# Spare TensorE matmuls in the waits of a decode attention block

## The chip, the cores and the metric

One core of a Trainium2 chip. The metric is device time in microseconds (us) of one execution. Each timed execution also has a *span*, from its first to its last recorded instruction, which lies 1.3 to 2.8 us below the time for most kernels here.

## The reference, cut to what matters

One token goes through a layer norm, attention over a cache of 65536 positions, and a gated feed-forward layer.

```
x: 1 x 512.  32 query heads, 8 heads of K and V, 65536 positions of 128 each, bf16
q = layernorm(x) @ wq
p = softmax(q @ K^T / sqrt(128));  o = p @ V       # 4 query heads share one head of K and V
h = x + o @ wo
out = h + (sigmoid(n @ w_gate) * (n @ w_up)) @ w_down,  n = layernorm(h)
```

K and V are 16.8 MB per head and cache, 268 MB in all. With the weights the kernel reads 282.33 MB once.

## The kernel before: the parts that matter

One queue (SP) issues every large load in a fixed order: K and V of each head in pieces, then wo, the last pieces of V, w_gate, w_up, w_down. A load waits only until its place in an SBUF ring is free. VectorE transposes K (`ktw`), TensorE makes the scores, then the sums with V in "rounds" of eight matmuls: four column groups of 32, two chunks of V.

```
def pv(h, r, rounds=0):                 # one round of V: 8 matmuls into bank PO
    for k in range(2):
        for tq in range(4):
            ... mm_at(e, ps(PO, 0, 512, 32*tq, 32*tq+32), PT_sb (registers), ring (registers), False, 32, 32*tq)

def pe_flow(e, section):                # TensorE's program is a loop over heads and blocks
    ...
    goto("part")
    e.br_eq(i, i_last, on_true="values", on_false="scores")     # the last head has no scores of a next head
    label("scores")
    ...
    e.br_eq(i, i_first, on_true="next", on_false="values")
    label("values", "part")
    e.reg_mov(m, PARTS[0])
    away("br_eq", w, w0, "values0", lambda: section("V0"), "sums")   # block 0: 10 rounds; block 3: 6 rounds
    ...
    section("B")                        # one round, then registers and branches
    e.reg_alu(p, p, s, ALU.add)
    ...
    away("br_eq", w, w0 - 12, "outs", lambda: section("O"))          # the head's output

# the end: projection of the last head, statistics, gate and up (32 matmuls), mask product, w_down (56 matmuls)
WD_SPLIT = [(0, 8), (8, 12), (12, 14)]  # w_down is loaded in three pieces: 32, 16 and 8 of the 56 matmuls
```

## Time and profile before

| | before |
|---|---|
| time, median of the first 3 runs | 658.21 us (658.2 to 658.58) |
| span of the profiled run | 656.0 us |
| mean granted TensorE clock | 0.770 |
| bytes read | 282.33 MB |

The page's busy times (engine, us, share of the span, instructions) and its two costliest matmul groups (line, engine, what; busy us, mean ns of one; idle time before them and what ended it):

```profile
PE 439.9 (67%) x2315; PEld 70.0 (11%) x1547; DVE 350.2 (53%) x432; ACT 42.8 (7%) x114; POOL 3.6 (1%) x17
...
L415 PE MATMUL PS<-ktw 128*128 128x512 bf16 x1024 | 293.5, 439 | 103.1 <-DVE ktw L496 96.7
L415 PE MATMUL PS<-ring,PT_sb 128*32 x1024 | 108.3, 517 | 66.5 <-PEq L171 36.7
```

No engine is busy for more than 67% of the span. The scores (first group) and the rounds of V (second) are all of TensorE's large work, and their mean durations mix fast and slow matmuls.

### The profile page before, as it was taken

How to read it: one execution, taken by the hardware profiler on the slowest of the kernel's cores; microseconds unless marked ns; L12 is line 12 of the kernel's file. 1: busy time of each engine (PE TensorE's matmuls, PEld its weight loads, DVE VectorE, ACT ScalarE, POOL GpSimd, SP SyncE). 2: the span in 40 equal slices, each digit the busy share in tenths (PEclk: the TensorE clock that was granted, in tenths of full speed). 3: DMA queues.
4: the chain of work that ended last, by engine and by line, in shares of the span. 5: the costliest groups of instructions: out<-in, count | busy, mean ns of one | idle time of the engine just before them, and what ended most of it. 6: DMA issues, size and time to landing. Idle time of an engine off the chain costs nothing. (4 is left out here: it accounts for less than half of the span.)

```text
span 656.0 us, 6289 instructions
## 1 busy us (share of the span) xinstructions
PE 439.9 (67%) x2315; PEld 70.0 (11%) x1547; DVE 350.2 (53%) x432; ACT 42.8 (7%) x114; POOL 3.6 (1%) x17
## 2 busy tenths in 40 slices
PE   0698577837678567766677467694767766765765
PEld 0200010101001010010100100010100101001222
DVE  2299846847266645637258380684536572573102
ACT  1100200020000200011000200002000020002001
POOL 1000000000000000000000000000000000000000
PEclk9979788768778577786597786776777956877677
DMA  9999999999999999999999999999999999999998
GB/s 400 432 448 432 432 416 435 432 447 430 448 432 432 432 418 439 447 441 429 418 448 432 432 428 444 444 444 432 402 446 432 432 432 432 464 432 412 422 431 351
DMA packets 8498, 282.33 MB, mean 430 GB/s; under 512 B 1073, under 2 KB 1074, under 8 KB 1586
## 3 DMA queue, kind: packets, MB, share of 16 engines
q1 hardware_dynamic: 8354, 282.33, 99.6%
q10 hardware_dynamic: 144, 0.00, 0.0%
HBM read 282.33 MB, written 0.00 MB: 430 GB/s over the span
## 5 line engine op out<-in xcount | busy, mean ns | idle before, releaser
L496 DVE STREAM_TRANSPOSE ktw<-ring 128x1024 f32<-128x1024 f32 x256 | 292.3, 1208 | 162.1 <-DMA ring<-in_A_k_cache_dram 162.1
L415 PE MATMUL PS<-ktw 128*128 128x512 bf16 x1024 | 293.5, 439 | 103.1 <-DVE ktw L496 96.7
L415 PE MATMUL PS<-ring,PT_sb 128*32 x1024 | 108.3, 517 | 66.5 <-PEq L171 36.7
L415 PEld LDWEIGHTS PS<-ktw 128*128 x256 | 27.2, 106 | 359.6 <-issue 255.9
L585 ACT ACTIVATE po_sb<-PS,rl 128x512 bf16<-128x512 f32 x8 | 5.5, 687 | 521.5 <-PE PS L415 521.5
L415 PEld LDWEIGHTS PS<-ring,PT_sb 128*32 x1024 | 21.7, 116 | 149.1 <-issue 147.4
L503 DVE TENSOR_REDUCE M_sb<-PS 128x1 f32<-128x512 f32 x32 | 19.9, 683 | 19.9 <-PE PS L415 19.9
L531 DVE TENSOR_REDUCE gmj<-PS 1x4 f32<-1x128 f32 x8 | 2.2, 279 | 44.2 <-PE PS L529 44.2
L542 ACT ACTIVATE P_sb<-PS,negmax 128x512 bf16<-128x512 f32 x32 | 21.5, 685 | 0.3
L552 DVE STREAM_TRANSPOSE PT_sb<-P_sb 128x512 bf16<-128x512 bf16 x32 | 20.1, 682 | 1.7 <-ACT P_sb L542 1.7
L386 PE MATMUL PS<-st,onesf 128*128 128x2 f32 x4 | 1.2, 363 | 17.1 <-DVE st L385 17.1
L601 DVE TENSOR_TENSOR Lw<-O,blk_of 128x896 bf16<-128x896 bf16 (+1 forms) x2 | 1.4, 682 | 19.2 <-ACT O L591 19.2
L415 PE MATMUL PS<-ring,xz 128*8 x32 | 9.0, 452 | 2.3 <-issue 2.3
L529 PE MATMUL PS<-identf,gm 128*1 128x128 f32 x16 | 4.5, 380 | 5.4 <-issue 3.3
L536 PE MATMUL PS<-one_f,gmrep 1*128 1x1 f32 x16 | 4.4, 345 | 5.0 <-DVE gmrep L533 5.0
L559 DVE TENSOR_REDUCE lsum<-PS 128x1 f32<-128x4 f32 x8 | 1.3, 162 | 11.3 <-PE PS L557 11.3
L415 PE MATMUL PS<-ktw,O 128*1 x26 | 7.2, 443 | 0.0
L542 ACT ACTIVATION_READ_ACCUMULATOR P_sb<-PS,negmax 128x1 f32 x32 | 6.5, 203 | 0.0
L401 DVE CAST hT<-x_col 128x4 f32<-128x4 bf16 x1 | 0.2, 170 | 11.7 <-DMA x_col<-in_A_x_dram 11.7
L588 PE MATMUL PS<-sel_bf,po_sb 128*128 128x4 bf16 x32 | 2.1, 171 | 6.3 <-ACT po_sb L585 6.3
L460 DVE STREAM_TRANSPOSE qt<-qh 32x512 bf16<-32x512 bf16 x1 | 0.7, 699 | 10.5 <-ACT qh L457 10.5
L557 PE MATMUL PS<-L_sb,lsel 128*128 128x4 f32 x16 | 2.5, 229 | 3.8 <-DVE PT_sb L552 3.8
(82 smaller groups left out, 69.5 us busy)
## 6 DMA issues: line engine op xcount, KB each, us to landing
ring<-in_A_k_cache_dram SPq DMA_DIRECT2D x16, 6144.0 KB, 24.3
ring<-in_A_v_cache_dram SPq DMA_DIRECT2D x15, 6144.0 KB, 25.7
ring<-in_A_v_cache_dram SPq DMA_DIRECT2D x9, 4096.0 KB, 30.1
ring<-in_A_k_cache_dram SPq DMA_DIRECT2D x8, 4096.0 KB, 24.7
ring<-in_A_wq_dram SPq DMA_DIRECT2D x1, 4096.0 KB, 12.1
ktw<-in_A_wo_dram SPq DMA_DIRECT2D x1, 3584.0 KB, 14.6
ring<-in_A_v_cache_dram SPq DMA_DIRECT2D x1, 2048.0 KB, 38.3
ring<-in_B_w_gate_dram SPq DMA_DIRECT2D x1, 1792.0 KB, 29.6
```

Source lines behind the costliest of these rows:

```text
L415: return e.add_instruction(mybir.InstMatmult(name=nc.get_next_instruction_name(), engine=mybir.EngineType.PE, ins=[rhs, lhsT], outs=[e.low ...
L496: op("dve", lambda e, d=dst, sr=src: e.transpose(d, sr), deps, f"T{b}.{c}", to="T")
L503: op("dve", lambda e, u=u: e.tensor_reduce(M_sb[:, u % 4:u % 4 + 1], ps(u % NS, 0, 512), AX.X, ALU.max), [f"S{b}.{NC - NR + k}"], f"mx{u}" ...
L529: op("pe", lambda e: e.matmul(ps(MISC, 0, 128, 0, 1), lhsT=gm[:, :], rhs=identf[:, :], start=True, stop=True), [f"gm{h}"], f"gmT{h}", to="Q")
L531: op("dve", lambda e: e.tensor_reduce(gmj[:, :], ps(MISC, 0, 128, 0, 1).rearrange("p (i a c) -> p a i c", a=4, c=NC), AX.XY, ALU.max), [f" ...
L536: op("pe", lambda e: e.matmul(ps(MISC, 128, 129), lhsT=gmrep[0:1, :], rhs=one_f[0:1, 0:1], start=True, stop=True), [f"gmrep{h}"], f"neg{h}")
L542: op("act", lambda e, b=b: e.activation(P_sb[:, (b % 4) * 512:(b % 4 + 1) * 512], ps(b % NS, 0, 512), AF.Exp, bias=negmax[:, k:k + 1], sca ...
L552: op("dve", lambda e, b=b: e.transpose(PT_sb[:, (b % 4) * 512:(b % 4 + 1) * 512], P_sb[:, (b % 4) * 512:(b % 4 + 1) * 512]), [f"E{b}"], f" ...
L557: op("pe", lambda e: e.matmul(ps(MISC, 132, 136), lhsT=lsel[:, :], rhs=L_sb[:, :], start=True, stop=True), [f"PT{NR * h + NR - 1}"], f"l{h ...
L585: op("act", lambda e: e.activation(po_sb[:, :], ps(PO, 0, 512), AF.Copy, scale=rl[:, :]), [f"PV{h}.{NR - 1}", f"rl{h}"], f"po{h}", to="po")
L588: op("pe", lambda e, t=t: e.matmul(ps(OX, 0, 4), lhsT=po_sb[:, t * 128:(t + 1) * 128], rhs=sel_bf[:, 8 * t:8 * t + 8:2], start=(t == 0), s ...
L601: op("dve", lambda e: e.tensor_tensor(Lw[i][:, :].rearrange("p (j c) -> p j c", j=n), bass.AP(tensor=O2, offset=j0, ap=[[NQ, 128], [1, n], ...
```

## The change

TensorE waits often, and its clock drops in the waits. The change runs spare matmuls whose result nobody reads (inputs `qz` and `ident`, output in bank 5), so that the clock stays full (*warm* below; *cold* is the half clock): one per round of V, three per block, two ahead of the output's copy, one behind it, one behind the last projection.

```
+        def warm(e, n=1, load=True):
+            for i in range(n):
+                more = dict(ldweights=False) if i or not load else {}
+                e.add_instruction(mybir.InstMatmult( ... ins=[qz[:, 0:504], ident[:, :]], outs=[ps(5, 0, 504)], ... **more))
 ...
             e.reg_mov(m, PARTS[0])
+            warm(e, 3)
             away("br_eq", w, w0, "values0", lambda: section("V0"), "sums")
 ...
             section("B")
+            mm_at(e, ps(5, 0, 504, 96, 128), PT_sb at reg 11, qz[:, 0:504], True, 32, 96, kept=True)
 ...
-            away("br_eq", w, w0 - 12, "outs", lambda: section("O"))
+            def outs():
+                warm(e, 2)
+                section("O")
+                warm(e, 1, load=False)
+            away("br_eq", w, w0 - 12, "outs", outs)
 ...
         project(range(NQ - GS, NQ), O3, ["O3.1", "wo1"], last=True)
+        op("pe", lambda e: warm(e, 1, load=False))
```

More of the change, by code (lines that the diff above doesn't have):

```diff
@@ L418, in mm_at @@
                 bass_skip_group_check=True, **more))
+        def warm(e, n=1, load=True):
+            for i in range(n):
+                more = dict(ldweights=False) if i or not load else {}
+                e.add_instruction(mybir.InstMatmult(
+                    name=nc.get_next_instruction_name(), engine=mybir.EngineType.PE, ins=[e.lower_ap(qz[:, 0:504]), e.lower_ap(ident[:, :])],
+                    outs=[e.lower_ap(ps(5, 0, 504))], start_tensor_calc=True, stop_tensor_calc=True, tile_size=(128, 128),
+                    tile_position=(0, 0), bass_skip_group_check=True, **more))
         regs, R, here = [], {}, OrderedEngineSet([mybir.EngineType.PE])
@@ L716, in pe_flow @@
             section("B")
+            mm_at(e, ps(5, 0, 504, 96, 128), at_reg(PT_sb, reg(e, 11), [[PT_ROW, 128], [4, 32]]), e.lower_ap(qz[:, 0:504]), True, 32, 96, kept=True)
             e.reg_alu(p, p, s, ALU.add)
```

## The prediction

> **What bounds the kernel now.** I read the page first: the DMA rows, then the clock row; then the chain that ended last in order of time; then the tail of the trace in narrow windows; last the waits of the DMA queue.
>
> The page's slices (40 equal parts, tenths) and its DMA queue:
>
> ```profile
> PEclk9979788768778577786597786776777956877677
> DMA  9999999999999999999999999999999999999998
> ...
> q1 hardware_dynamic: 8354, 282.33, 99.6%
> ```
>
> The DMA row is 9 in every slice but the last, while the clock row swings between 5 and 9. If TensorE's clock set the pace, the DMA row would dip where the clock dips. It does not. The windows view gives the rate (PE, PEld, DVE, ACT, POOL busy, granted clock, DMA share, GB/s):
>
> ```profile
> 60.00:640.00 580.00, 396.63 (x2048) 59.81 (x1350) 310.72 (x367) 35.72 (x100) 0.00 (x0) 0.75 1.00 433
> ```
>
> 433 GB/s with a DMA share of 1.00 over 580 us: there is no idle time of the DMA engines for a faster TensorE to fill. 282.33 MB at 433 GB/s is 652.0 us; the first bytes start about 1 us in, the last data stop at about 653.4 us, the span is 656.0 us, and the timed median of 658.21 us lies 2.2 us above that span. So time = stream + what hangs on its last piece. Only two things can matter: whether the stream ever starves, and the end.
>
> **The end.** The chain that ended last (start us, length us, what):
>
> ```profile
> 636.64 1.05 PE PS L415 x8
> ...
> 642.14 0.63 PE PS L415 x8
> 642.77 0.48 issue
> 643.25 0.66 PE PS L415 x8
> 643.90 0.02 issue
> 643.93 0.69 ACT po_sb L585
> ...
> 648.19 3.19 PE PS L801 x32
> 651.37 0.02 issue
> 651.40 0.93 DVE hh L811
> 652.32 0.02 issue
> 652.35 0.66 DVE hhT L814
> 653.00 0.04 issue
> 653.05 1.02 PE PS L819 x56
> ```
>
> It names TensorE, and a first look says that 17 us of chain from 636.64 could shrink if the clock were full. But the page's list of DMA issues gives the landing of the three pieces of w_down (KB, us from issue to landing); the timeline has them issued between 616.8 and 617.7:
>
> ```profile
> ring<-in_B_w_down_dram SPq DMA_DIRECT2D x1, 1024.0 KB, 35.1
> ...
> ring<-in_B_w_down_dram SPq DMA_DIRECT2D x1, 256.0 KB, 36.0
> ```
>
> The last is issued at 617.7 and lands at about 617.7 + 36.0 = 653.7. The 56 matmuls of line 819 come in groups of 32, 16 and 8 by piece. Narrow windows of that line alone (PE and PEld busy, clock, DMA share, GB/s):
>
> ```profile
> 653.70:653.75 0.05, 0.05 (x16) 0.00 (x0) 1.00 0.00 0
> 653.75:653.80 0.05, 0.05 (x16) 0.05 (x8) 1.00 0.00 0
> ```
>
> No weight is loaded from 653.70 to 653.75, then the last eight begin: the group that waits for the last piece. So the "chain" from hhT at 653.05 and the last landing at 653.7 meet within some hundredths of a us. A chain that is faster gains nothing; a chain that is slower by x adds nearly x. That asymmetry is the heart of this prediction.
>
> **What the Trainium skill says.** (1) "TensorE: Matmul & The Clock Gate", section "What's actually happening": the array's clock is halved after an idle window of about 3.4 us and full after a busy one; the windows run freely. This trace agrees: cut at that pitch, the clock reads 1.00 from 630.90 to 634.30, 0.51, 0.50, then 0.99 from 641.10, 0.50 for two, 1.00 from 651.40. The same page's "Why this matters for your kernels" advises leaving no idle gap over about 3 us: the idea behind the change. (2) "DMA: Bandwidth & Descriptors", "Where 436 GB/s comes from": 16 ports make 435.2 GB/s. The trace runs at 433, so the stream is at that ceiling. The page adds that the HBM side binds at about 358; this trace, with one core, exceeds it. (3) "TensorEngine Tiling (Array Packing)", "Instruction Overhead": each matmul carries some 60 cycles, so a spare is not free.
>
> **The change part by part.** Nothing is removed. It adds matmuls of 504 columns into bank 5, which the kernel otherwise uses only behind them on the same engine.
> - One per round of V: 8 heads x 16 rounds = 128, in column group 96 alone, with the weights already there. Three ahead of each block: 8 x 4 x 3 = 96. Two ahead of and one behind each head's output: 24. One behind the last projection. Sum 249.
> - Full 512-column matmuls take 375 to 632 ns in the records at full and half clock; the spacing of scores sharing a weight is about 0.22 us warm (four between weight loads 0.87 us apart at 42.60 and 43.47) and 0.43 cold (1.70 us). So a spare occupies 0.21 or 0.42 us: 52 to 105 us over the run, nearly all in waits (PE is busy 439.9 of 656).
> - A round of V is not clock-bound. Warm rounds start at 87.26, 88.43, 89.55, 90.71 (1.12 to 1.17 us apart, PE busy 0.63 in each); cold ones at 637.79, 638.90, 640.07 (1.11 and 1.17, busy 1.05). The rest is the sequencer: about 26 instructions in 1.13 us, 0.04 us each. A spare adds one instruction, about 0.04 us per round. Warm, it fits the 0.48 us gap. Cold, group 96 has three matmuls in a row, 3 x 0.42 = 1.27 us, which is 0.13 over the present spacing.
> - In the stream: the spares keep the rounds warm and the scores mostly so. I expect the mean clock to go from 0.77 to about 0.87 and the mean score matmul from 439 ns to 400 or less. Worth: zero, as the DMA share is 1.00. Nor does it starve: K pieces of 6144 KB (6.29 MB, 14.5 us at 433 GB/s) land 24.3 us after issue, so each is queued about 9.8 us ahead of its turn. The extra work ahead of a release is under about 1 us of rounds plus 1.3 us of spares.
> - In the tail: six rounds from 636.64, 6 x 0.04 = 0.24, and up to three cold rounds x 0.13 = 0.4: +0.6 at the output copy. Two spares ahead of that copy (0.4 warm) lie beside ACT's 0.69; the two later ones lie beside ACT and DVE work of 0.5 us or more. Then, if the clock stays full past 644.6 (estimate: two rounds with spares, 1.7 us, plus two spares, 0.4, fill 0.6 of that window, where 0.56 was enough at 333.9), the sixteen column matmuls (0.71) and the small ones save about 0.5: +0.1 at 648.2. Line 801, 3.19 cold, would take 1.6 warm, but its last piece of w_up lands only at about 649.4, and what it saves ends before w_down is there. Sum at the end: between -0.03 and +0.5 us, best guess +0.1.
>
> **Rivals.** (a) *The tail shrinks by 1.5 to 2 us*: for it, the chain is on TensorE at a clock of 0.50 from 644.6 to 651.4. Against, the last eight matmuls start with the last landing. It would make 656.5 if I misread the landing. (b) *The spares delay the releases and the stream starves*: for it, the queue's longest waits are for VectorE's markers (304.3 us) and TensorE (162.9 + 71.6). Against, the lead of about 10 us. If a hole of 0.5 us came per head: 662. (c) *The tail gets longer*: cold rounds with spares, and a clock that still falls before line 801. All of +0.6 kept gives 658.8. This is the likeliest miss. (d) *Scores faster, stream faster*: needs DMA idle time, and there is none; 0.
>
> **Range and chances.** Centre 658.3 = 658.21 + 0.1. The three runs before spread over 0.38 us; with a tail of -0.03 to +0.5 the range is 657.6 to 658.9. A change of 2% is 13 us, twenty times the range's reach: faster 0.01, same 0.98, slower 0.01.
>
> **What would show it.** Right: PE instructions 2315 + 249 = 2564; the clock about 0.87; score matmuls shorter; the DMA row still all 9 and the queue's share over 99%; the last group of w_down's matmuls still starting within 0.1 us of the last landing, with hhT done sooner or within 0.5 us. Rounds still 1.12 to 1.20 us apart. Wrong: a slice where the DMA row falls below 9 in the middle, a landing lead of K near 14.5 us (starved queue), or a stream rate other than 433 GB/s, which would mean that TensorE's reads of SBUF touch the transfers.

## The result and the profile after

| | before | changed |
|---|---|---|
| median of 6 runs each | 658.38 us (657.69 to 658.6) | 657.7 us (657.49 to 659.01) |
| ratio, 95% interval | | 0.9994 (0.9981 to 1.0007) |
| span of the profiled run | 656.0 us | 656.2 us |
| mean granted clock of that run | 0.770 | 0.872 |
| PE instructions | 2315 | 2564 |

The same, as predicted. The changed kernel's page, with the lines that answer to those of before:

```profile
PE 460.9 (70%) x2564; PEld 73.8 (11%) x1587; DVE 350.2 (53%) x432; ACT 42.9 (7%) x114; POOL 3.6 (1%) x17
...
PEclk9989799788889697896887988787978978879798
DMA  9999999999999999999999999999999999999998
...
q1 hardware_dynamic: 8354, 282.33, 99.6%
...
L415 PE MATMUL PS<-ktw 128*128 128x512 bf16 x1024 | 287.1, 430 | 103.2 <-DVE ktw L504 86.0
L415 PE MATMUL PS<-ring,PT_sb 128*32 x1024 | 90.5, 423 | 52.6 <-PEq L171 26.8
```

Its windows view from 60 to 640 us (PE, PEld, DVE, ACT, POOL busy, clock, DMA share, GB/s):

```profile
60.00:640.00 580.00, 416.90 (x2293) 63.80 (x1390) 311.49 (x368) 35.75 (x100) 0.00 (x0) 0.86 1.00 433
```

The clock did what the change wants: from 0.75 to 0.86 in this stretch, and a matmul of a round takes 423 ns instead of 517. The DMA row, the queue's share of 99.6% and the 433 GB/s are what they were. TensorE got faster at something that nobody waits for.

The end of the changed kernel, from its timeline (start us, us, engine, line, operation, operands, count, idle time before):

```profile
636.25 0.80 PE L423 MATMUL PS<-qz,ident 128*128 128x504 bf16 x3 [0.35 <-issue]
637.42 0.63 PE L415 MATMUL PS<-ring,PT_sb 128*32 x8 [0.37 <-issue]
637.89 0.38 PE L415 MATMUL PS<-qz,PT_sb 128*32 128x504 bf16 x1
638.53 0.63 PE L415 MATMUL PS<-ring,PT_sb 128*32 x8 [0.27 <-issue]
...
639.70 0.63 PE L415 MATMUL PS<-ring,PT_sb 128*32 x8 [0.32 <-issue]
...
644.72 0.69 ACT L593 ACTIVATE po_sb<-PS,rl 128x512 bf16<-128x512 f32 x1 [36.28 <-PE PS L415]
...
648.82 2.74 PE L817 MATMUL PS<-ring,hc 128*1 128x448 bf16 x32 [0.25 <-DVE hc L804]
...
653.25 1.01 PE L835 MATMUL PS<-ring,hhT 128*1 128x128 bf16 x56 [0.97 <-DVE hhT L830]
```

The last rounds of V begin at 637.42 instead of 636.64, behind the third group of three spares, and the copy of the output (ACT's `po_sb`) at 644.72 instead of 643.93: both 0.8 us late. Of this, 0.26 is a later landing of the last piece of V (635.96 before, 636.22 now, by the landing events of the packed traces); the rest is TensorE, which starts 1.20 us after that landing instead of 0.68. The rounds are warm (0.63 us busy each). From the first of the six to the copy pass 7.30 us with their spares; before, 636.64 to 643.93, it was 7.29 without. By the gate matmuls (L817) the lag is 0.63, as the statistics matmuls took 0.38 instead of 0.59; they end 0.2 us late, and so does `hhT`, the gated vector that w_down multiplies.

The span is 0.2 us longer as well, but this is the stream's doing. The last of the three pieces of w_down is issued at 619.2 and lands 34.8 us later, at 653.93; before, it landed at 653.71. The last eight matmuls start with it (timeline of the queue; landing; windows of line 835 as in the prediction):

```profile
618.23 2.97 SPq L355 DMA_DIRECT2D ring<-in_B_w_down_dram  x3
...
ring<-in_B_w_down_dram SPq DMA_DIRECT2D x1, 256.0 KB, 34.8
...
653.85:653.90 0.05, 0.05 (x20) 0.05 (x4) 1.00 0.00 0
653.90:653.95 0.05, 0.05 (x16) 0.00 (x1) 1.00 0.00 0
653.95:654.00 0.05, 0.05 (x16) 0.03 (x8) 1.00 0.00 0
```

So the prediction's own test held: the last eight start 0.04 us after the landing, in both kernels.

That is one execution. The six spans of the changed kernel lie between 656.1 and 656.6 us.

### The profile page after: what moved, and what is told of

It is laid out like the page before. It is cut to its first block, busy times and chain, and to the rows that moved or that the text cites. A ratio compares the mean times of both kernels' runs of the same rounds, so it can differ in the third digit from the quotient of the medians. Undisturbed runs are those within 1.5% of the kernel's fastest.

```text
span 656.2 us, 6578 instructions
## 1 busy us (share of the span) xinstructions
PE 460.9 (70%) x2564; PEld 73.8 (11%) x1587; DVE 350.2 (53%) x432; ACT 42.9 (7%) x114; POOL 3.6 (1%) x17
## 3 DMA queue, kind: packets, MB, share of 16 engines
q1 hardware_dynamic: 8354, 282.33, 99.6%
## 4 chain that ended last, share of the span: by engine, by line
DMA 54%; PE 26%; DVE 12%; issue 6%; ACT 1%; PEldq 0%; PEld 0%; SPq 0%
DMA ring<-in_A_k_cache_dram 33%; PE PS L415 22%; DMA ring<-in_A_v_cache_dram 19%; DVE ktw L504 11%; DMA x_col<-in_A_x_dram 2%; PE PS L423 2%; ACT P_sb L550 1%; PE PS L817 0%; DVE PT_sb L560 0%; DVE M_sb L511 0%; PE PS L660 0%; PEldq L171 0%; PE PS L835 0%; PE PS L386 0%; PE PS L544 0%
## 5 line engine op out<-in xcount | busy, mean ns | idle before, releaser
L504 DVE STREAM_TRANSPOSE ktw<-ring 128x1024 f32<-128x1024 f32 x256 | 292.3, 1207 | 152.2 <-DMA ring<-in_A_k_cache_dram 152.2
L415 PE MATMUL PS<-ktw 128*128 128x512 bf16 x1024 | 287.1, 430 | 103.2 <-DVE ktw L504 86.0
L415 PE MATMUL PS<-ring,PT_sb 128*32 x1024 | 90.5, 423 | 52.6 <-PEq L171 26.8
L415 PE MATMUL PS<-qz,PT_sb 128*32 128x504 bf16 x128 | 53.1, 415 | 0.0
L415 PEld LDWEIGHTS PS<-ring,PT_sb 128*32 x1024 | 25.0, 115 | 134.7 <-issue 131.0
L423 PE MATMUL PS<-qz,ident 128*128 128x504 bf16 x121 | 33.7, 374 | 2.1 <-issue 2.1
L423 PEld LDWEIGHTS PS<-qz,ident 128*128 128x128 bf16 x40 | 3.8, 96 | 35.3 <-issue 35.3
```

Of the source, the lines that this page charges most:

```text
L415: return e.add_instruction(mybir.InstMatmult(name=nc.get_next_instruction_name(), engine=mybir.EngineType.PE, ins=[rhs, lhsT], outs=[e.low ...
L423: e.add_instruction(mybir.InstMatmult(name=nc.get_next_instruction_name(), engine=mybir.EngineType.PE, ins=[e.lower_ap(qz[:, 0:504]), e.lo ...
L504: op("dve", lambda e, d=dst, sr=src: e.transpose(d, sr), deps, f"T{b}.{c}", to="T")
```

## The experiments

Theory: the stream of loads sets the time, with some 10 us of lead over the engines; what the spares win or lose inside it is hidden, and only the end counts, where the last landing of w_down is a floor. Rivals: each spare costs sequencer time (the prediction's 0.04 us per round); the warm tail is a real gain; the spares' gain is real everywhere and merely hidden by the stream; TensorE's extra reads slow the loads.

| run | edit | median us | before | ratio (95%) | spans of its runs | clock, profiled run |
|---|---|---|---|---|---|---|
| e1_rounds | only the spare per round | 657.84 | 658.66 | 0.9989 (0.9975 to 1.0002) | 656.2 to 656.9 | 0.821 |
| e2_blocks | only three per block | 658.61 | 658.66 | 1.0005 (0.9991 to 1.0018) | 656.4 to 657.6 | 0.796 |
| e3_ends | only those about the output | 658.65 | 658.66 | 1.0 (0.9986 to 1.0013) | 656.4 to 657.3 | 0.792 |
| e4_nolast | no groups in the last head | 657.8 | 658.66 | 0.9992 (0.9978 to 1.0005) | 656.0 to 657.0 | 0.867 |
| e5_block12 | twelve per block | 665.4 | 658.32 | 1.011 (1.0068 to 1.0151) | 659.1 to 662.9 | 0.902 |
| e6_few_v_before | before, V cut | 563.79 | 658.32 | 0.8563 (0.8547 to 0.8578) | 561.4 to 563.6 | 0.838 |
| e7_few_v_after | changed, V cut | 572.83 | 658.32 | 0.8708 (0.8693 to 0.8722) | 570.2 to 572.7 | 0.909 |
| e8_round4 | four per round | 661.13 | 658.32 | 1.0039 (1.0022 to 1.0056) | 659.3 to 663.7 | 0.887 |
| c1_before | before again | 658.16 | 658.52 | 0.9997 (0.9984 to 1.0011) | 656.2 to 656.6 | 0.793 |
| c2_after | changed again | 658.17 | 658.52 | 0.999 (0.9977 to 1.0004) | 656.0 to 656.8 | 0.870 |
| e9_tail | e4 and more spares in the tail | 661.25 | 658.52 | 1.0043 (1.003 to 1.0057) | 656.1 to 656.3 | 0.874 |
| e10_pad | changed, ten instructions more at the start | 661.19 | 658.13 | 1.005 (1.0037 to 1.0064) | 656.1 to 656.5 | 0.851 |

All give a correct result but e6 and e7, which cut the data (the comparison's tolerance passes them too: the attention's output is small beside x).

### One part at a time

e1 keeps only the spare in the round:

```
-            warm(e, 3)                                   # per block
-                warm(e, 2)                               # ahead of the copy
-                warm(e, 1, load=False)                   # behind it
-        op("pe", lambda e: warm(e, 1, load=False))       # behind the last projection
```

> Only the spare per round of V is kept (128 spares). Theory (the stream sets the time, the tail meets the last landing): DMA queue share over 99%, 433 GB/s in the middle; the rounds of the last piece of V start with its landing near 636.7 us, not at 637.4 as in the changed kernel, since the nine spares of the last head are gone; round spacing 1.11 to 1.17 us as without spares; mean clock 0.80 to 0.86; span 655.9 to 656.1 us. Rival of the prediction (an added instruction costs 0.04 us of sequencer per round): spacing 1.16 to 1.21 us, chain at the output copy later by 0.24 us, span 656.2 or more. Ratio to before in both: 0.999 to 1.001.

The rounds start at 636.84, 0.68 us after the landing as in the kernel before, and from the first of the six to the copy of the output pass 7.35 us, with one more matmul in each, against 7.29 in the kernel before (636.64 to 643.93): the 0.04 us of sequencer per spare, 0.24 in six rounds, falls. The rival's other sign, a copy 0.24 us later, did come (644.19 against 643.93), but 0.20 of it is the later landing. The clock fits (0.82). The profiled span does not, at 656.9, and the trace says why: the clock was 0.50 from 647 us to the end, and the w_down matmuls took 1.66 us instead of 1.0. The other four spans lie between 656.2 and 656.5, also above the 655.9 to 656.1 expected.

e2 keeps only `warm(e, 3)`, e3 only the four lines about the output:

> Only the three spares ahead of each block are kept (96). Theory: stream untouched; in the last head the three groups of three stand in a row between the rounds of the first piece and those of the last, so these start at 636.7 to 637.2 us; mean clock 0.77 to 0.83, as most rounds go cold; span 656.0 to 656.3 us. Rival (the rounds' spares, not the groups, made the 0.79 us delay): the last rounds start with the landing at 636.6 to 636.7 us exactly as before.

> Only the spares about the output (two ahead of each copy, one behind, one behind the last projection: 25). Theory: they lie beside work of ACT and DVE and shift nothing: last rounds start at 636.6 us, copy at 643.9 us, hc within 0.1 us of 647.97 (before), span 655.9 to 656.1 us, mean clock 0.76 to 0.79. Rival (these spares are what shortens the tail): the 32 gate matmuls end 0.5 us or more earlier than 651.34; even then the span stays, as the last weights land at 653.7 us.

In e2 the groups of three end at 635.1 and the rounds start at 637.16 after a wait of 2.03 us, so the groups alone cause no delay; the spans missed the 656.0 to 656.3 expected. Neither run differs from the kernel before (ratios 1.0005 and 1.0). In e3 the rounds start at 636.78, near the 636.6 expected, but the last two ran cold, copy and `hc` came 0.5 us late (644.47 and 648.51), and the span of 657.2 missed: here the whole tail was cold. Its w_down line in the timeline:

```profile
653.58 1.66 PE L833 MATMUL PS<-ring,hhT 128*1 128x128 bf16 x56 [0.97 <-DVE hhT L828]
```

Against 0.99 us busy in the kernel before's first trace: the same 56 matmuls cost 0.67 us more when the clock is halved there, and none of it is a wait for the last landing (653.84).

e4 moves the three spares into the score blocks, which the last head does not have:

```
-            warm(e, 3)                       # at label "values"
+            warm(e, 3)
             e.br_eq(i, i_first, on_true="next", on_false="values")
```

> The groups of three are moved to the score blocks, so that the last head (no scores) has none. Theory: the 0.79 us by which the last rounds of V start late came from the nine spares of the last head with their three branches; without them these rounds start with the landing at 636.6 to 636.8 us, hhT is done by 653.1 us, and the last eight matmuls start within 0.06 us of the last landing; span 655.9 to 656.1 us, 0.1 to 0.3 under the changed kernel. Rival: without the nine the clock halves in the wait, cold rounds with a spare take 1.27 us each, and the gain is lost: span 656.3 us or more.

The rounds start at 636.86 after a wait of 3.95 us. The rival's clock came true, its price did not: three of the six rounds ran cold (1.05 us and more busy), but the pause of 2 us ahead of the fifth round took up the lag, and the copy starts at 644.18, 7.32 us after the first round. hhT is done by 653.03, the last eight matmuls start at about 653.84, some 0.1 us later than in the kernel before and, as there, 0.04 us after their piece has landed; the span is 656.0. The other four spans (656.3 to 657.0) are above the 655.9 to 656.1 expected. The nine spares of the last head stood in the way in the changed kernel's first trace, but they need not: in c2_after, with them, the rounds start at 636.85.

### Does the tail depend on chance?

> The kernel before once more, unchanged, for a second trace and for the scatter of its span. Theory (the tail depends on where the free-running clock windows fall, and the trace on record caught a lucky phase): spans scatter over 656.3 to 657.7 us with a mean near 657.0, and where the span is 657 or more the last 56 matmuls take about 1.66 us at a clock of 0.50 instead of 1.0. Rival (the chip of an hour ago was merely slower): all spans within 0.3 us of 656.0.

> The changed kernel once more, on the same chip. Theory (its spares make the tail's clock steadier): mean span 656.1 to 656.5, 0.4 to 0.9 us under that of the kernel before in this call, and a narrower scatter. Rival (no difference but chance between sessions): means within 0.2 us of each other.

c1's own five spans lie between 656.2 and 656.6, while the nine runs of the identical kernel that served as its "before" scatter from 656.3 to 657.6, with a mean of 656.92. So the scatter is there and the slow side was not caught in a trace of this kernel: that its runs above 657 us had a cold tail, as e1 and e3 had, is likely but not shown. Over all of these experiments the kernel before gave 39 spans with a mean of 656.83 us (656.1 to 657.7), the changed one 11 with a mean of 656.28 (656.0 to 656.8). That is 0.5 us or 0.08%; the timed ratios (0.9994 and 0.999, both with 1 inside the interval) do not resolve it. The expectation's own comparison is as open: c2's mean lies 0.64 us under the nine runs of before, as expected, but 0.16 under c1's five, as the rival has it.

The changed kernel's second trace shows both sides of the chance in one tail:

```profile
648.25 1.73 PE L817 MATMUL PS<-ring,hc 128*1 128x448 bf16 x32 [0.26 <-DVE hc L804]
...
652.64 1.70 PE L835 MATMUL PS<-ring,hhT 128*1 128x128 bf16 x56 [2.25 <-DVE hhT L830]
```

Here the gate matmuls ran warm, 1.73 us against 2.74 in the first trace, and hhT came 0.6 us sooner. But the w_down matmuls could not finish before w_down was there, and TensorE, by then waiting, fell to 0.50 at 653.2 us. The span is 656.3: a whole microsecond won in the gate matmuls and nothing at the end.

### Is the last landing a floor?

e9 adds more spares to e4's tail: three instead of two ahead of the copy, three instead of one behind it, and

```
-        op("pe", lambda e: warm(e, 1, load=False))       # behind the last projection
+        op("pe", lambda e: warm(e, 2, load=False))
+        op("pe", lambda e: warm(e, 1))                   # behind the statistics
+        op("pe", lambda e: warm(e, 3, bank=7))           # behind the mask product
```

> Groups of three as in the run without them in the last head; in the tail three spares instead of two ahead of the copy, three instead of one behind it, two behind the last projection, one behind the statistics, and three into bank 7 behind the mask product. Theory (the end is bound by the last landing near 653.7 us once the chain is fast): the 32 gate matmuls take 1.6 to 2 us instead of 2.7 to 3.15, hhT is done by 652.0 us, the last eight matmuls start with the landing; span 655.8 to 656.1, scatter under 0.4 us; so no more than 0.3 us under the changed kernel. Rival (the chain was the bound all along): hhT earlier by 1 us makes the span 655.2 or less. Third: the spares delay the chain: 656.5 or more.

Its timeline:

```profile
648.32 1.68 PE L818 MATMUL PS<-ring,hc 128*1 128x448 bf16 x32
...
652.72 0.98 PE L837 MATMUL PS<-ring,hhT 128*1 128x128 bf16 x48 [1.66 <-DVE hhT L832]
653.92 0.28 PE L837 MATMUL PS<-ring,hhT 128*1 128x128 bf16 x8 [0.23 <-DMA ring<-in_B_w_down_dram]
```

Now the profile names the floor itself: 48 matmuls are done, TensorE idles for 0.23 us, and the last eight start on the landing of w_down's last piece. With everything warm the span is 656.1 to 656.3 us. The expectation put hhT at 652.0 and it came at 652.7, but the verdict stands: the end is the landing plus 2.2 us, and no spare moves it.

The other traces agree. Their landing events give when the last piece of w_down landed (us):

| trace | last piece lands | last eight matmuls start, after the landing | span minus landing |
|---|---|---|---|
| before | 653.71 | 0.04 | 2.26 |
| changed | 653.93 | 0.04 | 2.26 |
| e2_blocks | 654.18 | 0.04 | 2.25 |
| e4_nolast | 653.79 | 0.04 | 2.26 |
| c1_before | 654.00 | 0.04 | 2.25 |
| c2_after (w_down partly cold) | 653.92 | 0.04 | 2.35 |
| e9_tail | 653.88 | 0.04 | 2.25 |
| e10_pad (below) | 653.89 | 0.05 | 2.25 |
| e1_rounds (w_down cold) | 653.90 | 0.63 | 2.98 |
| e3_ends (w_down cold) | 653.84 | 0.98 | 3.34 |

In the first eight the last matmuls start with the landing and the span follows it; the landing itself scatters over 0.47 us, with spares and without. The cold tails of e1 and e3 add 0.7 and 1.1 us. So a span above some 656.5 is likely a cold tail, but the executions without a trace do not show it. (In e5 and e8, below, the last piece lands at 654.13 and 653.99.)

What nobody expected is the time: 661.25 us, 5.0 to 5.5 above the span. e10 tests whether the length of TensorE's program does it. It leaves the changed kernel as it is and puts ten instructions at the very start, in a wait of over 10 us:

```
+        op("pe", lambda e: warm(e, 9), ["ident", "qz0"])
         ln_stats(0, lambda e: e.tensor_copy(hT[0][:, :], x_col[:, :]), "x", 0, 0)
```

> The changed kernel with nine more spares at the very start, while TensorE waits for its first input (some 12 us), so ten more instructions in its program and none of them on a path. The run with the longer tail program had a span of 656.2 us but a time 5.0 to 5.5 us above the span, where the others have 1.3 to 2.7. Theory (the longer program of TensorE as such costs time outside the span): time minus span 5 us or more, span as that of the changed kernel (656.1 to 656.8), time near 661.3 us. Rival (it is what the added spares do at the end): time minus span stays 1.3 to 2.7 us and the time near 657.8 us.

Spans of 656.1 to 656.5, times of 661.11 to 661.66, 4.9 to 5.5 above the span. So instructions that cost nothing inside the span cost some 3.5 us outside it (5.1 on average, against 1.65 in the eleven runs of the changed kernel). e9 has ten TensorE instructions more than the changed kernel, e5 nine (three of its four runs are 5.0 or more above the span, one is 2.0), e8 three (1.4 to 1.7). Somewhere between three and nine more there is a step. The traces show one thing that goes with it: in six of them (changed, c1, c2, e5, e9, e10) the DMA view of the microseconds behind the span has a transfer of 16384 bytes of kind "instruction", which starts 1.3 to 1.9 us after the end of the span, and in the other eight it has none there. The six are the profiled executions with 2.05 us or more between span and time, the eight those with 1.73 or less. What makes 5 us of 2 to 2.8, no trace here shows, and why one run of e5 escaped the step stays open.

### How much lead does the stream have?

e5 has `warm(e, 12)` for `warm(e, 3)`. e8 has four spares per round for one.

> Twelve spares instead of three ahead of each block: 27 more in the last head's three empty blocks, 9 x 4 x 0.21 = 7.7 us more per head. Theory: the stream's lead of some 10 us hides the heads (DMA queue share over 98%, middle at 432 to 433 GB/s), and only the tail pays: the last rounds of V start 27 x 0.21 = 5.7 us later plus up to 1.9 us for the first block, span 661 to 664 us. Rival (the stream starves as soon as the releases slip): a hole of several us per head, middle at 425 GB/s or less, span 670 us or more. Rival (TensorE's reads of SBUF slow the transfers): the rate falls though no hole shows.

> Four spares per round instead of one, all in column group 96. If a round is bound by the sequencer with 0.04 us per instruction: spacing 1.13 + 3 x 0.04 = 1.25 us. If the array binds: six matmuls in a row in group 96, 6 x 0.21 = 1.28 us warm. If the sequencer's time is in its branches and register work and issue overlaps: 1.13 would stay, but the array forbids it. In the tail six rounds cost 0.7 to 0.9 us more: span 656.8 to 657.4 us; the stream untouched (433 GB/s).

In e5 the middle still runs at 433 GB/s with TensorE at 77% busy, and the last piece of w_down lands at 654.13, no later than in e2. The span is 659.1 in the trace, the fastest of the four runs (659.1 to 662.9; two lie in the 661 to 664 expected). Neither a starved stream nor slower transfers in this trace: only the end moved, as 36 spares in a row (7.83 us) now stand ahead of the last rounds, which start at 641.16. So the rival that TensorE's reads of SBUF slow the loads falls as well. The median of 665.4 also holds the step of e10.

e8's rounds (every line is one round or its spares):

```profile
645.75 0.64 PE L415 MATMUL PS<-ring,PT_sb 128*32 x8
646.18 1.01 PE L415 MATMUL PS<-qz,PT_sb 128*32 128x504 bf16 x4
647.03 0.63 PE L415 MATMUL PS<-ring,PT_sb 128*32 x8
```

Rounds 1.28 us apart: six matmuls in a row in column group 96, at 0.21 each, as the array's side of the expectation had it, against 1.25 for the sequencer's side; the single spare of e1, which added 0.06 us in six rounds, decides between them. The spans (659.3 to 663.7, the trace is the slowest) missed the 656.8 to 657.4 expected: I had counted only the last six rounds. In the last head TensorE works in one chain from the last scores on, ten more rounds, projection and groups included, and the last rounds started at 644.42, 7.0 us later than in the changed kernel.

### Would the spares pay where the stream is not the bound?

Both kernels with V loads cut to two chunks each, read again by every round. The result is wrong; TensorE does the same matmuls, the bytes fall to 174 MB.

```
+            if k == "V":
+                a, z = (j0 + 10, j0 + 12) if q == 0 else (a, a + 2)
...
+            e.reg_alu(v, v, 10 * 2 * CH, ALU.add)
...
+                e.reg_mov(v, addr_of(ring, AT["V7"][1] * CH))
+                pv_regs(e)
...
-            e.reg_alu(v, v, 2 * 2 * CH, ALU.add)
+            e.reg_alu(v, v, 0, ALU.add)
```

> The kernel before with each load of V cut to two of its chunks, and the rounds reading those again: wrong result on purpose, same instructions on TensorE, 174 instead of 282 MB. The stream no longer fills the time: at 433 GB/s it needs 403 us, PE is busy for about 400. Theory: the engines now set the pace, 430 to 480 us, DMA share 0.85 to 0.95. This is the base for the next run.

> The changed kernel with the same cut of V (wrong result on purpose). Theory A (the spares' gain is real and only hidden by the stream): faster than the cut kernel before by 1% or more. Theory B (where TensorE is the bound it is busy and warm by itself, so that the spares only cost: up to 12 x 0.21 = 2.5 us per head): slower by 1 to 5%. My guess is B, +2%.

The cut kernel before takes 563.79 us, not the 430 to 480 expected: I had set the busiest engine as the pace, but VectorE and TensorE wait for each other block by block (VectorE 23.3 us in all, TensorE 53.4), and VectorE still waits 41.9 us for K. The DMA row of the page shows that the stream no longer fills the time (its queue is busy for 75.1%, not the 85 to 95 expected):

```profile
DMA  9999819886696939795897839694897839608930
```

The changed kernel with the same cut takes 572.83 us: 1.6% slower (572.97 over 563.83, the means), at a clock of 0.91 instead of 0.84. So the stream hid no gain of the spares as a whole: 9.1 us over eight heads is 1.1 us per head lost, of the 3.2 us that fifteen spares outside the rounds occupy (3 x 4 + 3, at 0.21 each). Spares in the rounds and spares ahead of the blocks were not tested apart here, and VectorE still waits for K in both (41.9 and 48.2 us), so that the loads still have a part in the pace.

## Why the prediction was right, and where its steps were not

**The bound: right.** "There is no idle time of the DMA engines for a faster TensorE to fill" held in every run with the full data: 433 GB/s in the middle from a TensorE busy 66% to 78%. Rival (b) fell with e5, where 7.7 us more per head starved nothing (last landing at 654.13), and rival (d) with the changed kernel, where matmuls 94 ns shorter in the rounds left the rate as it was.

**The clock: right, but for the scores.** 249 spares gave 2564 instructions and 0.872 where 0.87 was expected. The mean score matmul did not follow: 430 ns, not 400 or less. Scores wait for transposes, and these for K (152.2 us on VectorE in the page after); three spares do not bridge waits of that size, which is the likely reason.

**"A spare adds one instruction, about 0.04 us per round": wrong.** Six rounds took 7.30 to 7.35 us to the copy in the six traces with one spare each (changed, c2, e1, e4, e9, e10) and 7.27 to 7.29 in three without (before, c1, e2; in e3 the last two rounds ran cold): at most 0.08, not 0.24. The estimate divided the spacing of a round by its instructions, as if the time were spread over them evenly. The spare costs next to nothing until its column group is full (e8: 1.28 us with four).

**The tail sum: in its range by luck, wrong in its terms.** I expected 0.24 for instructions and 0.4 for cold rounds, +0.6 at the copy. The trace has +0.8 there, with no slower round in it: 0.26 is the later landing of V, and for the rest TensorE came late to the last rounds, from a serial last head with three groups of spares in it (e4 removes this). The savings that I expected behind it came in part: 0.2 at the statistics and 0.45 in the gate matmuls, but nothing in the sixteen column matmuls, which I had counted in (0.70 against 0.69). The span ended 0.2 us up, in the predicted -0.03 to +0.5, but because the last piece of w_down landed 0.22 us later, which the sum does not contain. The medians went the other way, to 657.7 against 658.38, close to the lower edge of the range.

**"A chain that is faster gains nothing; a chain that is slower by x adds nearly x": the first half right, and the trace behind it an unrepresentative one.** e9 shows the floor at 656.1, and eight of ten traces end on theirs. But the trace of before, at 656.0, was already on that floor, below every later span of that kernel, and the mean of the later 39 spans is 656.83. I took one trace's tail for the kernel's tail, and set its span beside the median of other executions (the "2.2 us above that span"; the profiled one itself took 657.36, 1.36 above). Where the clock drops in the tail differs from trace to trace (at 644.6 before, 649.3 changed, 653.3 in c2), and a cold end costs up to 0.7 us in the w_down matmuls alone. So the change may give some tenths of a us, in the steadier tail; e1 and e4, which keep the spares in the rounds, have mean spans of 656.4 against 657.1 in the same call for before, e2 and e3 (without them) 657.1. But c1, the kernel before itself, also reached 656.4. Five spans do not settle this, and the timed difference stays unresolved.

**The Trainium skill on the waits.** "TensorE: Matmul & The Clock Gate", "Why this matters for your kernels", asks for no idle gap over about 3 us between bursts of matmuls, and the spares work towards that (clock 0.770 to 0.872). Its table of goals does not ask first whether anybody waits for the matmuls, and that was the whole question here. "Perfetto Trace Analysis", "What "DMA-bound" means", lists what can bind such a kernel instead; its first case, the DMA engines themselves, is this one (queue busy for 99.6%).

## What to carry to other kernels

Before warming an engine, look whether the stage is bound by it: a DMA row of 9 in every slice and a rate at its ceiling say that the clock is free to drop. A chain that ended last and a last landing can coincide; find the one instruction that waits for the landing before counting what the chain could save. And do not build a tail model on one trace where the clock's drops fall differently from run to run: compare the spans, and the last landings, of several runs first.

## What the Trainium skill lacked or had wrong

- "DMA: Bandwidth & Descriptors", "Where 436 GB/s comes from", says that for transfers between HBM and SBUF the HBM side binds at about 358 GB/s. With one core running, 580 us of this kernel go at 433 GB/s, right at the page's other number of 435.2. ("Perfetto Trace Analysis", "Roofline", has this right: it lets a single core of trn2 go over 358, up to its DMA engines' 435 or so.)
- "TensorE: Matmul & The Clock Gate", "What's actually happening", names an idle window as what halves the clock. Here a window that was far from idle did: in the changed kernel's first trace PE is busy 2.03 of 3.41 us from 645.87 to 649.28 (half of its 33 matmuls one column wide), and the clock is halved from there on; yet behind 639.05 to 642.46, with 2.02 us busy in matmuls of 504 and 512 columns, it stayed full. In the kernel before 3.21 of 3.4 us from 648.0 to 651.4 gave it back. What counts as busy, and how much is enough, is not on the page.
- The same page's "Why this matters for your kernels": the goals are matmul throughput and no drops in it; what filling the gaps can cost is not there. With less to load (e6 and e7, queue busy for 75%), the clock rose from 0.84 to 0.91 and the time by 1.6%.
- "TensorEngine Tiling (Array Packing)", "Instruction Overhead", gives each matmul some 60 cycles, without saying when they are hidden. One more matmul in each of six rounds of eight left their time at 7.30 us against 7.29.
- "Runtime: NRT & Kernel Launch", "Instruction fetch mechanics", has programs fetched in blocks of 16 KiB, at a cost that is mostly hidden. That a longer TensorE program can cost time outside the recorded instructions, in a step, is not there: ten instructions more raised the time from 1.3 to 2.8 us above the span to 4.9 to 5.5 above it, at an unchanged span. Whether such a block is the step is not shown.
